# Set places for the norms' transposes in a two-layer transformer block: pairs, a second queue for the first group's reads, and dummy matmuls at the start

## The chip, the cores and the metric

The kernel runs on one core of a Trainium2 chip. The metric is the device time of one execution in microseconds (us); the number given for a kernel is the median of its runs. The engines are TensorE (matmuls, transposes), VectorE, ScalarE, GpSimd and SyncE, which issues transfers. ScalarE and GpSimd can issue transfers too. In the profile they are called PE (PEld is its weight load), DVE, ACT, POOL and SP; a "q" behind the name marks the issuing of transfers.

## The reference

Two layers, each an attention block and an MLP, with shared weights. The sequence has 2048 rows of 512 numbers, 32 heads of 16, a hidden width of 1792.

```python
def attn(x, wqkv, wo):                      # on the normed x
    qkv = (x @ wqkv).reshape(B, S, 3, H, Dh).transpose(2, 0, 3, 1, 4)
    q, k, v = qkv[0], qkv[1], qkv[2]
    p = softmax(einsum("bhqd,bhkd->bhqk", q, k) * Dh ** -0.5)
    o = einsum("bhqk,bhkd->bhqd", p, v)
    return o.transpose(0, 2, 1, 3).reshape(B, S, D) @ wo

def mlp(x, w1, b1, w2):                     # on the normed x; Mish
    h = x @ w1 + b1
    return (h * tanh(softplus(h))) @ w2

for layer in range(2):
    x = x + attn(layernorm(x), wqkv, wo)
    x = x + mlp(layernorm(x), w1, b1, w2)
```

## The kernel before

The 2048 rows are cut into NCH = 4 chunks of CW = 512. Each layer has three stages.

**Projections** (`qkv`, `v_parts`). The normed chunk is needed transposed (512 features in four blocks of 128 partitions). To keep precision, an operand is split into a high part (a copy by ScalarE) and a low part (a subtraction), and a product is three matmuls (`mm3`, L176 to L178): high by high, low by high, high by low, for each of four blocks, twelve matmuls for one projection of 128 output rows by 512 columns. There are 32 projections (m, c) per layer: m = 0 to 3 are q, m = 4 to 7 are k, c is the chunk. Their order is the list `order`. Each goes into one of three PSUM banks with the tag "s"; ScalarE and VectorE empty it into `pt` (`split_psum`, L170 and L171), and ScalarE issues a write of 512 KB to `scr` in DRAM (L479). The v products follow, interleaved with the first maxima of the attention.

**Norms** (`norm_parts`). For a chunk: statistics of four tiles (`bn_stats`, `bn_aggr`, L191 and L192, VectorE), the power -0.5 (L188, GpSimd), and for each tile of 128 rows the scaled `xn` (L204, VectorE), four transposes (L215, TensorE) into a PSUM tile, and the split into `th` and `tl` (L170, L171). In the first layer's projections and for the last chunk of the second layer's, the PSUM tile has the tag "mx", in the MLP "acc" or "s". `xn` takes a buffer with the tag "f" (two), which it shares with the MLP's `hb`. The first layer's norms are written out before the projections, the second layer's last one (`late`) just before the first projection that needs it.

**Attention** (`Attention`). `prep_qk(g)` reads a group of four heads from `scr` into two tiles `ks` and two tiles `qs`: 24 reads of 128 KB (L266) and four small ones of a constant (`minus`, L259). For the first group all 28 are issued at once when the eight projections with m = 0 and 4 are done, half by SP and half by GpSimd. Then a loop of 512 steps works through scores, exponentials, products with v, and the maxima of the next group.

**MLP** (`mlp`). Loop over chunks and 14 blocks f of the hidden width: `hid` makes twelve matmuls and a chain over ScalarE, VectorE and GpSimd (`hb`, `he`, `hr`, `ah`, `al`, L602 to L612), `outp` makes the twelve matmuls of the second product two steps later (LAG = 2). `hooks` puts the norms of other chunks (`spread`), the last output projection (`quarter`) and loads at given (c, f).

The order on an engine is chosen by the tile framework's scheduler, except for instructions pinned by `behind` (they stay in program order) and TensorE's instructions that go through `att.pe` with `chained` set (each depends on the one before). Before, `chained` is set once the first group's reads are issued. Buffers come from pools; an instruction waits until its buffer is free.

Of the kernel before, what the change touches and what calls it, by code (L numbers as in the profile page):

```python
# [43 lines left out]
KEEP = 2  # L44
GSTEPS = NCH * NKT
# [21 lines left out]
def kernel(ctx: ExitStack, tc: tile.TileContext, x, wqkv, wo, w1, b1, w2, out):  # L67
# [23 lines left out]
    nc.sync.dma_start(b1t, b1.rearrange("(f p) -> p f", p=P))  # L91
# [33 lines left out]
    def split_load(key, src, a, b, later, raw=None):  # L125
        t = b8([P, 2, a, b], F32R, "s" + key)
        if raw is None:
            raw = tmp.tile([P, a, b], F32, tag="raw", name="r" + key, bufs=3)
        behind(nc.sync.dma_start(raw, src))

        def split():
            behind(nc.scalar.activation(t[:, 0], raw, AF.Copy))
            behind(nc.gpsimd.tensor_tensor(t[:, 1], raw, t[:, 0].bitcast(F32), op=ALU.subtract))
            unkept.append((key, t))

        later.append(split)
        return t
# [42 lines left out]
    def norm_parts(src, nm, got, key, tag, fine=False, pin=lambda ins: ins, pe=lambda ins: ins, halves=False):  # L180
# [20 lines left out]
        for t in range(NCH):  # L201
            xn = t512("f", f"xn{nm}{t}")
# [7 lines left out]
            if tag == "mx":  # L210
                tp = ps.tile([P, 2, 512], F32, tag=tag, name=f"tp{nm}{t}")[:, 0]
            else:
                tp = pbank(tag, f"tp{nm}{t}")
            for k in range(KT):
                pe(nc.tensor.transpose(tp[:, ts(k, P)], xn[:, ts(k, P)], ident))  # L215
# [3 lines left out]
    def norm(src, nm, got, key, tag, fine=False):  # L219
        for _ in norm_parts(src, nm, got, key, tag, fine):  # L220
            pass
# [6 lines left out]
    class Attention:  # L228
# [20 lines left out]
        def prep_qk(self, g):  # L249
            l = self.l  # L250
            ks, qs = [], []
            for u in range(HG // 2):
# [3 lines left out]
                for e in range(2):  # L256
                    r0 = e * HALF
                    queue = nc.gpsimd if g == 0 and e else nc.sync
                    queue.dma_start(  # L259
                        k[r0 + KROWS : r0 + MROWS].bitcast(F32).rearrange("p (r n) -> p r n", n=P),  # L260
                        minus[:, None, :].to_broadcast([MROWS - KROWS, S // P, P]),
                    )
                    yield
                    for t, parts, base in ((k, K_PARTS, NCH), (q, Q_PARTS, 0)):
                        for j, a in enumerate(parts):
                            queue.dma_start(  # L266
                                t[r0 + j * DH : r0 + (j + 1) * DH].bitcast(F32),
                                self.scr[base + m][a, (h0 + e) * DH : (h0 + e + 1) * DH, :].bitcast(F32),
                            )
                            yield  # L270
# [163 lines left out]
    def load_qkv(l, wts, which, later):  # L434
        raw = None
        for j in which:
# [3 lines left out]
            elif j < 4:  # L440
                wts[j] = split_load(key, *cols(wqkv, j), later)
# [5 lines left out]
    def qkv(l, wts, tt, order, late, due):  # L447
        scr = [dram.tile([2, P, S], F32R, name=f"scr{l}{m}") for m in range(2 * NCH)]
        att = Attention(l, scr)
# [9 lines left out]
        spare = []  # L459
        for n, (m, c) in enumerate(order):  # L460
            if c not in tt:
                late()
# [6 lines left out]
            else:  # L469
# [3 lines left out]
            mm3(  # L473
                acc,
                [(w[:, 0, k, ts(m % 2, P)], w[:, 1, k, ts(m % 2, P)], th[:, k], tl[:, k]) for k in range(KT)],
                pe=att.pe,
            )
# [20 lines left out]
        return att  # L498
# [90 lines left out]
    def mlp(l, x2s, w1t, w2t, tts, dst, hooks):  # L589
        acts, obs = {}, {}  # L590

        def hid(c, f):
# [62 lines left out]
    wts, tt, late = {}, {}, None  # L655
# [11 lines left out]
    load_qkv(0, wts, (0, 2), splits)  # L667
    xc.append(load_x(1))
    for c in range(NCH):
        parts = norm_parts(xc[c], f"q0{c}", tt, c, "mx", c == 0)  # L670
        next(parts)
        if c == 0:
            split_all(splits)
        for _ in parts:
            pass
        if c + 2 < NCH:
            xc.append(load_x(c + 2))
    for l in range(2):
        due = {}
        if l == 0:  # L680
# [8 lines left out]
        att = qkv(l, wts, tt, order, late, due)  # L689
# [80 lines left out]
        for c in range(NCH - 1):  # L770
            spread(hooks, [(c, f) for f in (range(8, 13) if c == 0 else range(5, 10))], x2s[c + 1], f"m{l}{c + 1}", tts, c + 1)
# [8 lines left out]
        if l == 0:  # L780
            late = lambda: norm(x2s[last], f"q1{last}", tt, last, "mx", True)
# [29 lines left out]
```

## Time and profile before

| | |
|---|---|
| median of 3 runs | 3584.75 us (3584.71 to 3588.09) |
| profiled execution | 3589.2 us, of which its span 3587.4 us |
| TensorE busy | 3540.3 us, 99% of the span |
| VectorE, ScalarE, GpSimd busy | 83%, 70%, 15% |
| first layer: norms and projections | 0 to about 145 us |
| first layer: attention, output projection | to about 1468 us |
| first layer: MLP | 1469 to about 1827 us |
| second layer: projections | from about 1800 to 1970 us |
| second layer: attention, output projection | to about 3250 us |
| second layer: MLP and end | to 3587.4 us |

How to read the profile: times are microseconds from the span's start. In a timeline, a line has the start, the time, the engine, the source line, the operation, output <- input, and in brackets the idle time of the engine before it and what ended that. A windows table gives for each stretch its length, then for each engine the busy time and the number of instructions, the granted clock of TensorE, and the mean share of the 16 DMA engines that was busy. A matmul's listed time contains its drain; in a stream, the distance of the starts is what it costs. Idle time of an engine that does not set the end costs nothing.

### The profile page before, as it was taken

What the parts mean: (1) busy time and instruction counts of PE and PEld (TensorE: products, weight loads), DVE (VectorE), ACT (ScalarE), POOL (GpSimd) and SP (SyncE); (2) the same over time, 40 slices, a digit from 0 to 9 for tenths busy, and PEclk for the clock granted to TensorE, in tenths of its full rate; (3) what the DMA queues carried; (4) which work ended last, traced back from release to release, by engine and by line L of the source; (5) the groups of instructions that cost most, each with busy time, mean ns of one, the idle gap of its engine ahead of it and who ended that gap; (6) DMA issues with size and microseconds to landing.
All of it is one profiled execution on the core that took longest, in us unless ns stands there. A gap on an engine that the chain in (4) does not pass through costs nothing.

```text
span 3587.4 us, 69160 instructions
## 1 busy us (share of the span) xinstructions
PE 3540.3 (99%) x28704; PEld 1942.6 (54%) x28704; DVE 2967.9 (83%) x3042; ACT 2518.1 (70%) x3411; POOL 550.4 (15%) x591
## 2 busy tenths in 40 slices
PE   7999999999999999999999999999999999999999
PEld 5644444444444444778776444444444444448887
DVE  4779999999999994666648799999999999946565
ACT  2178888888888888344421788888888888873444
POOL 2200000000010002444421000000000000024455
PEclk9999999999999999999999999999999999999999
DMA  6561322213121224500164312112021221245000
GB/s 193 195 170 39 81 54 68 61 46 79 45 67 51 52 79 70 181 36 13 47 183 165 70 32 40 32 41 38 26 47 29 46 38 29 79 73 178 36 12 24
DMA packets 139457, 255.11 MB, mean 71 GB/s; under 512 B 29432, under 2 KB 73336, under 8 KB 125320
## 3 DMA queue, kind: packets, MB, share of 16 engines
q1 hardware_dynamic: 112648, 175.64, 19.8%
q0 software_dynamic: 8224, 35.21, 3.5%
q10 hardware_dynamic: 18272, 39.85, 3.0%
q8 instruction: 225, 3.69, 0.5%
q14 instruction: 88, 0.72, 0.1%
HBM read 149.43 MB, written 100.14 MB: 70 GB/s over the span
## 4 chain that ended last, share of the span: by engine, by line
PE 49%; DVE 1%; DMA 1%; ACT 1%; issue 0%; POOL 0%; POOLq 0%; DVEq 0%; ACTq 0%; SPq 0%
PE pv L377 15%; PE pm L303 9%; PE ss L361 6%; PE sp L351 5%; PE mo L178 2%; PE h L176 2%; PE h L178 2%; PE h L177 2%; PE mo L176 2%; PE mo L177 2%; PE qk L176 1%; PE qk L178 1%; PE qk L177 1%; PE va L176 0%; DMA ks<-scr 0%
## 5 line engine op out<-in xcount | busy, mean ns | idle before, releaser
L307 DVE TENSOR_REDUCE mxv<-pm 128x2 f32<-128x1024 f32 x2048 | 2386.0, 1218 | 138.4 <-PE pm L303 87.6
L352 ACT ACTIVATE p<-sp 128x1024 f32<-128x1024 f32 x1366 | 1395.8, 1022 | 20.1 <-PE sp L351 14.1
L377 PE MATMUL pv<-p,va 128*32 128x256 f32 (+2 forms) x16032 | 1167.0, 392 | 0.1
L303 PE MATMUL pm<-ks,qs 48*128 48x512 f32 x4096 | 1097.1, 447 | 0.3
L362 ACT ACTIVATE p<-ss 128x512 f32<-128x512 f32 x1364 | 814.6, 597 | 348.5 <-PE ss L361 264.7
L351 PE MATMUL sp<-qs,ks 50*128 50x512 f32 x2732 | 726.5, 447 | 0.3
L377 PEld LDWEIGHTS pv<-p,va 128*32 128x32 f32 x16032 | 368.4, 109 | 498.3 <-issue 420.7
L303 PEld LDWEIGHTS pm<-ks,qs 48*128 48x128 f32 x4096 | 450.6, 184 | 345.1 <-issue 210.8
L361 PE MATMUL ss<-qs,ks 50*128 50x512 f32 x1364 | 611.3, 448 | 0.0
L361 PEld LDWEIGHTS ss<-qs,ks 50*128 50x128 f32 x1364 | 252.2, 185 | 329.3 <-ACT p L362 224.1
L351 PEld LDWEIGHTS sp<-qs,ks 50*128 50x128 f32 x2732 | 261.8, 183 | 200.8 <-ACT p L352 119.5
L322 POOL CAST np<-nt 128x32 fp32r<-128x32 f32 x64 | 13.3, 208 | 2214.2 <-DVE nt L320 2214.2
L608 POOL TENSOR_TENSOR hb<-hb,he 128x512 f32<-128x512 f32 x112 | 157.6, 1407 | 193.0 <-DVE he L605 189.0
L611 POOL TENSOR_TENSOR hb<-hb,hr 128x512 f32<-128x512 f32 x112 | 159.8, 1427 | 138.5 <-DVE ah L610 130.8
L606 ACT ACTIVATE hr<-he 128x512 f32<-128x512 f32 x112 | 70.8, 633 | 149.9 <-POOL hb L611 76.8
L612 DVE TENSOR_TENSOR al<-hb,ah 128x512 fp32r<-128x512 f32 x112 | 107.9, 963 | 81.9 <-POOL hb L611 80.5
L170 ACT ACTIVATE pt<-qk 128x512 fp32r<-128x512 f32 x64 | 37.9, 598 | 159.5 <-PE qk L178 133.5
L604 ACT ACTIVATE he<-he 128x512 f32<-128x512 f32 x112 | 70.8, 632 | 100.1 <-DVE he L603 97.0
L602 ACT ACTIVATE hb<-h,b1t 128x512 f32<-128x512 f32 x112 | 76.7, 685 | 77.0 <-DVE al L612 46.9
L610 DVE TENSOR_TENSOR ah<-hb,hr 128x512 fp32r<-128x512 f32 x112 | 76.9, 687 | 60.3 <-ACT hr L607 42.6
L605 DVE SCALAR_TENSOR_TENSOR he<-he 128x512 f32<-128x512 f32 x112 | 79.9, 714 | 42.0 <-ACT he L604 39.4
L603 DVE TENSOR_SCALAR he<-hb 128x512 f32<-128x512 f32 x112 | 69.7, 622 | 49.4 <-POOL hb L608 36.7
(224 smaller groups left out, 3246.7 us busy)
## 6 DMA issues: line engine op xcount, KB each, us to landing
scr<-pt ACTq DMA_DIRECT2D x64, 512.0 KB
qs<-scr SPq DMA_DIRECT2D x180, 128.0 KB
ks<-scr SPq DMA_DIRECT2D x180, 128.0 KB
vscr<-v SPq DMA_DIRECT2D x32, 512.0 KB
va<-vscr SPq DMA_DIRECT2D x64, 256.0 KB
oscr<-ot SPq DMA_DIRECT2D x64, 256.0 KB
ww<-sw POOLq DMA_DIRECT2D x14, 1024.0 KB, 4.5
num<-oscr SPq DMA_DIRECT2D x64, 128.0 KB
```

Of the source, the lines that this page charges most:

```text
L176: pe(nc.tensor.matmul(acc, ah, bh, start=first and i == 0, stop=False))
L177: pe(nc.tensor.matmul(acc, ah, bl, start=False, stop=False))
L178: pe(nc.tensor.matmul(acc, al, bh, start=False, stop=last and i == n - 1))
L303: nc.tensor.matmul(pm[:, e], qs[u][rows, q0 : q0 + P], ks[u][rows, ts(n, 512)], start=True, stop=True)
L307: nc.vector.tensor_reduce(self.mxs[b][:, 2 * u : 2 * u + 2, qt, n], pm, axis=AX.X, op=ALU.max)
L351: self.pe(nc.tensor.matmul(sp[:, e], k, q, start=True, stop=True))
L352: nc.scalar.activation(self.pts[-1][:, 0:n], sp[:, 0:n], AF.Exp, scale=SCALE)
L361: self.pe(nc.tensor.matmul(sp, k, q, start=True, stop=True))
L362: nc.scalar.activation(self.pts[i // 3][:, 2], sp, AF.Exp, scale=SCALE)
L377: nc.tensor.matmul(self.accs[b][ts(h, VW), cols], self.va[b // NCH][:, kt, h, :], self.pts[j][:, e, cols], start=kt == 0 and q0 == 0, stop ...
L608: nc.gpsimd.tensor_tensor(hb, hb, e, op=ALU.mult)
L611: nc.gpsimd.tensor_tensor(hb, hb, r, op=ALU.mult)
```

## The change

- `norm_parts` with the tag "mx" first makes all four `xn` (two in "f", two in "ah"), then transposes tiles in pairs into both halves of a PSUM tile, and splits a pair by one ScalarE and one VectorE instruction. With the tag "acc" `xn` takes a buffer with the tag "raw".
- The first layer's norms 1 to 3 and the second layer's last norm are called piece by piece at set places (n, k) of the projections, n counting them and k the four blocks inside one. TensorE's instructions are chained from the start of each layer's projections. The second layer's order has one more projection, (5, 1), before (0, 3).
- `prep_qk(0)` issues the 14 transfers of the first pair of heads at once (half by SP, half by GpSimd), the 14 of the second by ScalarE, pinned, two behind each of the next seven projections.
- Four dummy matmuls of zeros (f32, 128 x 512) before the first norm's transposes, three after them.
- The low parts of the first two weight tiles are made by VectorE instead of GpSimd; all of x is loaded right after them; `b1t` is loaded behind x.
- In the MLP the norm of chunk 1 lies at f = 0 to 4 instead of 8 to 12; the transposes of chunk 0's MLP norm lie two to five steps later in the output projections; in the last two f of the last chunk VectorE does two products that GpSimd did.

```diff
+PREP = 7
+WARM = (4, 3)
...
+        def scaled(t, tag):
+            if tag == "raw":
+                xn = tmp.tile([P, 2, 512], F32, tag=tag, name=f"xn{nm}{t}", bufs=3)[:, 0]
+            else:
+                xn = t512(tag, f"xn{nm}{t}")
             pin(
                 nc.vector.tensor_scalar(
                     xn, src[:, t], mv[:, t, 0:1], rs[:, t : t + 1], op0=ALU.subtract, op1=ALU.mult
                 )
             )
+            return xn
+
+        if tag == "mx":
+            xns = [scaled(t, ("f", "ah")[t // 2]) for t in range(NCH)]
+            yield
+            for u in range(NCH // 2):
+                tp = ps.tile([P, 2, 512], F32, tag=tag, name=f"tp{nm}{u}")
+                for e in range(2):
+                    for k in range(KT):
+                        pe(nc.tensor.transpose(tp[:, e, ts(k, P)], xns[2 * u + e][:, ts(k, P)], ident))
+                two = ts(u, 2 * P)
+                split_psum(
+                    th[:, :, two].rearrange("p k (t n) -> p k t n", n=P),
+                    tl[:, :, two].rearrange("p k (t n) -> p k t n", n=P),
+                    tp.rearrange("p t (k n) -> p k t n", n=P),
+                    pin,
+                )
+                yield
+            return
+        for t in range(NCH):
+            xn = scaled(t, "raw" if tag == "acc" else "f")
...
-                    queue = nc.gpsimd if g == 0 and e else nc.sync
-                    queue.dma_start(
+                    queue = nc.sync
+                    pin = lambda ins: ins
+                    if g == 0 and u:
+                        queue, pin = nc.scalar, behind
+                    elif g == 0 and e:
+                        queue = nc.gpsimd
+                    pin(queue.dma_start(
...
-            if c not in tt:
-                late()
+            for fn in within.get((n, 0), []):
+                fn()
...
+            for k in range(KT):
+                for fn in within.get((n, k), []) if k else []:
+                    fn()
+                mm3(
...
             for fn in due.get((m, c), []):
                 fn()
+            for _ in range(2):
+                next(parts, None)
             if m in (0, 4):
                 done += 1
                 if done == 2 * NCH:
-                    for _ in att.prep_qk(0):
-                        pass
-                    att.chained = True
+                    parts = att.prep_qk(0)
+                    for _ in range(2 * PREP):
+                        next(parts)
...
-            nc.gpsimd.tensor_tensor(hb, hb, e, op=ALU.mult)
+            mul = nc.vector if (l, c) == (1, NCH - 1) and f >= FT - 2 else nc.gpsimd
+            mul.tensor_tensor(hb, hb, e, op=ALU.mult)
...
-            nc.gpsimd.tensor_tensor(hb, hb, r, op=ALU.mult)
+            mul.tensor_tensor(hb, hb, r, op=ALU.mult)
...
-    load_qkv(0, wts, (0, 2), splits)
-    xc.append(load_x(1))
-    for c in range(NCH):
-        parts = norm_parts(xc[c], f"q0{c}", tt, c, "mx", c == 0)
-        next(parts)
-        if c == 0:
-            split_all(splits)
-        for _ in parts:
-            pass
-        if c + 2 < NCH:
-            xc.append(load_x(c + 2))
+    load_qkv(0, wts, (0, 2), splits, nc.vector)
+    xc += [load_x(c) for c in range(1, NCH)]
+    nc.sync.dma_start(b1t, b1.rearrange("(f p) -> p f", p=P))
+    att = attention(0)
+    att.chained = True
+    norms = [norm_parts(xc[c], f"q0{c}", tt, c, "mx", c == 0, behind, att.pe) for c in range(NCH)]
+    warm = b8([P, CW], F32, "warm")
+    nc.vector.memset(warm, 0.0)
+
+    def warm_up(i, n):
+        acc = pbank("s", f"warm{i}")
+        for _ in range(n):
+            att.pe(nc.tensor.matmul(acc, warm[:, 0:P], warm, start=True, stop=True))
+
+    warm_up(0, WARM[0])
+    for i in range(4):
+        next(norms[0])
+        if i > 1:
+            splits.pop(0)()
+    warm_up(1, WARM[1])
...
+            for c, (n0, n1, n2) in enumerate(((0, 0, 2), (2, 3, 5), (4, 6, 7)), 1):
+                for at in ((n0, 0), (n1, 0), (n2, 1), (n2, 3)):
+                    within.setdefault(at, []).append(lambda c=c: next(norms[c]))
         else:
-            order = [(0, 0), (0, 1), (0, 2), (4, 0), (4, 1), (4, 2), (1, 0), (1, 1), (1, 2), (5, 0), (0, 3), (4, 3)]
+            order = [(0, 0), (0, 1), (4, 0), (4, 1), (1, 0), (0, 2), (4, 2), (1, 1), (1, 2), (5, 0), (5, 1), (0, 3), (4, 3)]
+            att = attention(1)
+            att.chained = True
+            late = norm_parts(x2s[NCH - 1], f"q1{NCH - 1}", tt, NCH - 1, "mx", True, pe=att.pe)
+            for at in ((4, 0), (4, 0), (9, 0), (9, 2)):
+                within.setdefault(at, []).append(lambda: next(late))
...
-            for n in range({0: 1, 6: 1, 9: 2, 12: 2, 15: 2}.get(i, 0)):
+            for n in range({0: 1, 8: 1, 11: 2, 14: 2}.get(i, 0)):
                 next(first)
         for i, _ in enumerate(project(2)):
-            if i == 1:
+            for n in range({1: 2, 6: 1}.get(i, 0)):
                 next(first)
...
-            spread(hooks, [(c, f) for f in (range(8, 13) if c == 0 else range(5, 10))], x2s[c + 1], f"m{l}{c + 1}", tts, c + 1)
+            spread(hooks, [(c, f) for f in (range(5) if c == 0 else range(5, 10))], x2s[c + 1], f"m{l}{c + 1}", tts, c + 1)
...
-            late = lambda: norm(x2s[last], f"q1{last}", tt, last, "mx", True)
```

More of the change, by code (lines that the diff above doesn't have):

```diff
@@ L123, in keep, with split_load @@
         behind(nc.gpsimd.dma_start(kept[key].bitcast(F32), t.bitcast(F32)))
-    def split_load(key, src, a, b, later, raw=None):
+    def split_load(key, src, a, b, later, raw=None, low=nc.gpsimd):
         t = b8([P, 2, a, b], F32R, "s" + key)
@@ L132, in split @@
             behind(nc.scalar.activation(t[:, 0], raw, AF.Copy))
-            behind(nc.gpsimd.tensor_tensor(t[:, 1], raw, t[:, 0].bitcast(F32), op=ALU.subtract))
+            behind(low.tensor_tensor(t[:, 1], raw, t[:, 0].bitcast(F32), op=ALU.subtract))
             unkept.append((key, t))
@@ L432, in run, with load_qkv @@
             open_banks()
-    def load_qkv(l, wts, which, later):
+    def load_qkv(l, wts, which, later, low=nc.gpsimd):
         raw = None
@@ L445, in load_qkv, with attention, qkv @@
                 wts[j] = split_load(key, *rows2(wqkv[:, 2 * D : 3 * D], j - 4), later, raw[:, j - 4])
-    def qkv(l, wts, tt, order, late, due):
-        scr = [dram.tile([2, P, S], F32R, name=f"scr{l}{m}") for m in range(2 * NCH)]
-        att = Attention(l, scr)
+    def attention(l):
+        return Attention(l, [dram.tile([2, P, S], F32R, name=f"scr{l}{m}") for m in range(2 * NCH)])
+    def qkv(l, att, wts, tt, order, within, due):
+        scr = att.scr
         ahead = [0]
@@ L653, in load_x @@
         return xc
-    wts, tt, late = {}, {}, None
+    wts, tt = {}, {}
     splits, later = [], []
```

37 lines of the change are left out of this document (14 added, 23 removed).

## The prediction

> **What bounds the kernel now.** I read the page, then the windows of the projection stages, then the timeline and the chain where TensorE idles.
>
> ```profile
> span 3587.4 us, 69160 instructions
> PE 3540.3 (99%) x28704; PEld 1942.6 (54%) x28704; DVE 2967.9 (83%) x3042; ACT 2518.1 (70%) x3411; POOL 550.4 (15%) x591
> ```
>
> TensorE bounds it: all its idle time together is 3587.4 - 3540.3 = 47.1 us. The change removes no matmul of the result, so it can win only those 47.1 us and the slow matmuls behind idle stretches.
>
> ```profile
> core 0: us, PE busy (x) PEld busy (x) DVE busy (x) ACT busy (x) POOL busy (x), PEclk, DMA share, GB/s
> 33.00:51.00 18.00, 12.81 (x57) 9.83 (x57) 12.20 (x27) 6.04 (x12) 1.77 (x2) 0.81 0.10 36
> 81.20:90.30 9.10, 4.89 (x13) 3.83 (x13) 1.98 (x3) 3.57 (x5) 3.84 (x3) 0.63 1.04 173
> 1750.00:1800.00 50.00, 47.25 (x213) 36.16 (x212) 27.42 (x50) 23.82 (x38) 20.77 (x17) 1.00 0.12 43
> 1840.00:1850.00 10.00, 7.33 (x29) 5.46 (x29) 4.37 (x7) 2.77 (x5) 0.00 (x0) 0.75 0.27 105
> 1870.00:1880.00 10.00, 7.39 (x33) 5.76 (x32) 2.08 (x3) 2.06 (x4) 1.89 (x2) 1.00 1.02 256
> ```
>
> The idle time lies in five places: 13.1 us in the first 20 us (windows 0 to 10 and 10 to 20), 5.5 at 33 to 51, 4.2 at 81 to 90, 7.4 over the first layer's MLP (1460 to 1840), 5.3 at 1840 to 1880. The two attention loops, 160 to 1400 and 1980 to 3180, have almost none, and the program built from the changed kernel has TensorE's order unchanged in them.
>
> ```profile
> 17.17 1.65 PE L176 MATMUL qk<-thq,sqkv 128*128 128x512 f32 x3 [0.69 <-ACT thq L170]
> 37.10 1.09 PE L215 MATMUL tpq<-ident,xnq 128*128 128x128 f32 x4 [2.34 <-DVE mvq L192]
> 83.57 0.37 ACTq L479 DMA_DIRECT2D scr<-pt  x1
> 85.41 0.80 PE L176 MATMUL qk<-thq,sqkv 128*128 128x512 f32 x1 [4.21 <-DVE pt L171]
> 1799.66 0.50 PE L176 MATMUL qk<-thq,qkv0l 128*128 128x512 f32 x1 [0.33 <-ACT hb L602]
> 1844.44 1.68 PE L215 MATMUL tpq<-ident,xnq 128*128 128x128 f32 x8 [1.99 <-DVE tlq L171]
> 1860.45 11.46 DMA ks<-scr
> 1873.78 0.50 PE L176 MATMUL qk<-thq,qkv1l 128*128 128x512 f32 x1 [2.61 <-DVE pt L171]
> 3580.34 0.50 PE L178 MATMUL mo<-w26l,al 128*128 128x512 f32 x1 [0.90 <-DVE al L612]
> ```
>
> The brackets give the wait and its releaser. Transposes wait for a norm (37.10, 1844.44); projections wait for a bank that ScalarE and VectorE have not emptied (85.41, 1873.78), because ScalarE stood before issuing a write (83.57; its evacuation at 73.08 was the last before) while the first group's 24 reads of ks and qs crowd the DMA engines. After idle stretches matmuls step by 0.43 us instead of 0.227 for some 4.9 us (85.41 to 90.27): 12 of them lose 12 x 0.2 = 2.4 us.
>
> **Start and the first layer's norms.** Before, the first qk matmul runs at 17.17 and full speed begins at 22.31, when 11 are done: as if a full-speed run began at 22.31 - 11 x 0.227 = 19.8. After, I lay the built order end to end: x's last tile is reduced as now by 9.0, less 0.45 for the b1t issue that SP no longer makes first (row at 0.74), so the four xn (0.46 apart) end at 10.6. The first pair goes through transposes and ScalarE by 11.4, the weights' high part (1.06) by 12.4, the second pair by 13.5. VectorE does tl (1.22, taken from L587's 128x1024 row), the weights' low part (1.2 by the same row; GpSimd took 2.49 each), and the second tl by 15.1. Full speed from 14.9: 4.9 won.
>
> The dummies are f32 of 512 columns. The nearest row is pv 128x512 f32, 1.06 us with its drain: some 0.85 to 1.06 us at full step, 1.7 at half, so the first four run from about 1.3 to 7.2, and the transposes come at 9.2, 2.0 us later. Whether the speed survives is open: 1.99 us idle lost it at 1844.44 (eight transposes 1.68 us against 1.04), 2.61 us at 1871 to 1873.78 did not. If lost, transposes and the three later dummies run slow and full speed starts at 16.0: 3.8 won. I take 4.4.
>
> The Trainium skill ("TensorE: Matmul & The Clock Gate", Part 1: The HAM clock gate) says that the clock falls back only after at least one idle window of about 3.4 us, free-running. By that rule the 2.0 us would keep the speed and the gain would be 4.9; the 1.99 us row speaks against the rule as stated.
>
> From 17.17 to 81.2 TensorE does 17 projections, 204 x 0.227 = 46.3, and 48 transposes at 0.13, 6.2: 52.5 of 64.0 us. So 11.5 are lost, 2.6 of them the start above (19.8 - 17.17); 8.9 remain. After, norms 1 to 3 are placed at projections 0 to 7, transposes four steps of TensorE ahead of use. VectorE then carries, per chunk, statistics 2.46 + 0.5, xn 1.9, tl 2.5, and 0.69 per projection: 3 x 7.4 + 9 x 0.69 = 28.3 us inside nine projections with transposes (9 x 2.72 + 6.2 = 30.7). That nearly fills it. Laid end to end, chunk 1's first xn comes at 22.9 when TensorE arrives at 21.0: a wait of 1.9, and behind it (TensorE is in order) stand all projections. Later ones fit. Gain 8.9 - 1.9 = 7.0; 4.6 if that wait also brings the slow step back (2.4), 8.9 if there is no wait. The rows of 1.99 and 2.61 us leave this open; I take off a quarter of the 2.4: 6.4.
>
> **The reads.** Before: 4.2 idle + 2.4 slow at 81 to 90, and 2.6 at 1873. After, half of the 28 issues (24 reads, 4 of minus) are made at once by SP and GpSimd, the other 14 by ScalarE, two after each of the next seven projections, pinned in its order. An issue costs ScalarE some 0.37 (the ACTq row): 14 x 0.37 = 5.2 us in seven projections of 2.72 (19.0), beside evacuation and write, 7 x 1.0; it has room. Queued behind a waiting read are the evacuation of the next projection and its write; TensorE has two spare banks, 5.4 us. In the built program each transfer waits for the one eight before it. Reads cost the DMA engines about 0.7 us each (70 to 80: 2.22 MB at share 0.93, less about 1 MB of writes at the 395 GB/s of the window 17.17 to 22.31), two plus a write of 512 KB (1.3) make 2.7 us per projection: just as much as there is. So ScalarE will be held now and then; I expect 0.5 to 1 us lost per layer. Gain (6.6 - 1) + (2.6 - 0.5) = 7.7; ends 0 and 9.2, and below nothing by rival 1.
>
> **Second layer's last norm.** Its statistics move ahead of projection 4, its transposes into projection 9, so nothing waits: the 1.99 + 0.69 idle, 0.6 of slow transposes and 11 slow matmuls (2.2) go: 5.5, with 4 as the low end if two transposes wait.
>
> **MLP.** xn takes its buffer from "raw" instead of the two "f" buffers of hb. The 0.33 us waits for hb, one per step in the last chunk (1766 to 1800), are hb waiting for a buffer. TensorE loses 7.4 us over this MLP, with 0.6 to 1.4 us waits for al among them, which stay. The first chunk's norm now lies at f 0 to 4, beside num and ol (2.3 to 2.5 us each on VectorE), where there was no TensorE idle in 1460 to 1540: cover that it may use up. I take 3.5 of 7.4, from -2 to 6. In the second layer 0.7 (the wait at 3338), from -1.
>
> **Rest.** Transposes of chunk 0's MLP norm are moved two to five steps later in the output projections: waits of 0.59 + 0.56 and 0.63 + 0.56: 1.5 of 2.3; no loss, since nine of project(2)'s sixteen steps of 0.68 us still lie between the last and the first h. Tail: two products by VectorE (0.69 after ah's row) instead of GpSimd (1.30) in the last two f: up to 0.9, the wait at 3580.34, down to -0.5, since VectorE now does them in series; I take 0.6, nearer the row. Norm transposes in pairs halve the count of ScalarE and VectorE instructions but not their elements: nothing.
>
> **Sum.** 4.4 + 6.4 + 7.7 + 5.5 + 3.5 + 0.7 + 1.5 + 0.6 = 30.3 us. The profiled execution took 3589.2 (span 3587.4 + 1.8), 0.12% above the median of 3584.75; differences in span carry over, so from the median: 3584.75 - 30 = 3555. All low ends: 3.8 + 4.6 + 0 + 4 - 2 - 1 + 0 - 0.5 = 8.9, so 3576; all high: 4.9 + 8.9 + 9.2 + 5.5 + 6 + 0.7 + 2.3 + 0.9 = 38.4, so 3546.
>
> **Rivals.** (1) ScalarE's reads block its evacuations, and the kernel gets slower. Before, SP needed 16.08 us for six reads of ks (1860.10), 2.7 each. At that price 14 reads take ScalarE 38 us, with its own 7 a total of 45 against a cover of 19.0 + 5.4: TensorE loses 20 us a layer and 2.4 of slow steps, 45 in both layers, in place of the 9.2 lost now. The other gains are 30.3 - 7.7 = 22.6, so 3584.75 - 22.6 - 9.2 + 45 = 3598. It turns the sign from 2 x loss - 9.2 = 22.6, a loss of 16 us a layer, 2.2 us a read. Against it: those six stood behind all 24 issued in 5 us; now they come two per projection. 6%. (2) The reads take just as long and the same gaps stay (7.7 lost from the sum): 3562. For it: the DMA share is already 1.04 at 81 to 90, and the bytes are the same. 15%. The Trainium skill ("DMA: Bandwidth & Descriptors", Issuing engines are not separate DMA queues) says that transfers of all issuers run on the same 16 engines and another issuer saves only issue time; by that rule alone this rival would be the forecast, but the spreading in time is not an issuer's doing. (3) VectorE becomes the bound: the wait of 1.9 cools the array and recurs at chunks 2 and 3 (6.4 becomes 0), and the MLP gives nothing (3.5): 3565. 15%. (4) The dummies do not keep the clock: only the 0.6 between 4.4 and 3.8. This is inside the forecast.
>
> **Numbers.** Forecast 3555, chance 60%; (2) and (3) 15% each, (1) 6%, about no change 4%. From 3546 to 3572 holds the forecast, (2), (3) and most sums with several low ends; left out are (1), no change and the ends together. 0.2%, 7.2 us, is about what a measurement here tells from no change: faster 0.90, same 0.04, slower 0.06.
>
> **What would show it.** First qk matmul at full step by 15 to 16 us; no gap over 2 us at 33 to 51; no gap over 1 us at 70 to 95, and ScalarE's idle there under 5 us at a time; no transposes waiting at 1840; hb's 0.33 waits gone. It is wrong if ScalarE stands over 10 us in front of a read, or if the MLP's idle grows.

## The result and the profile after

The changed kernel takes 3556.12 us (median of 6 runs, 3554.26 to 3558.21), the kernel before 3585.06 in the same comparison (6 runs, 3583.44 to 3588.09): a ratio of 0.9917, 95% interval 0.9905 to 0.993, 28.9 us less. The forecast was 3555, the range 3546 to 3572. The profiled execution of the changed kernel took 3554.46.

The page of the changed kernel, span and busy times:

```profile
span 3552.7 us, 69170 instructions
PE 3531.6 (99%) x28718; PEld 1938.4 (55%) x28718; DVE 2963.1 (83%) x3039; ACT 2520.7 (71%) x3401; POOL 521.6 (15%) x571
```

TensorE's idle time is 3552.7 - 3531.6 = 21.1 us, where it was 47.1. Its busy time fell by 8.7 although the dummies add 8.1 of it: fewer matmuls run at the slow step (0.43 us from start to start, where the full step is 0.227), and short delays, which count as busy, went too (see the first MLP below).

The windows of the changed kernel, at the places of the forecast and at one that the forecast had not named (1515 to 1530; the row 70 to 90 covers the forecast's 81 to 90):

```profile
core 0: us, PE busy (x) PEld busy (x) DVE busy (x) ACT busy (x) POOL busy (x), PEclk, DMA share, GB/s
33.00:51.00 18.00, 18.00 (x95) 15.18 (x94) 12.04 (x20) 7.02 (x10) 1.77 (x2) 1.00 0.44 166
70.00:90.00 20.00, 19.34 (x85) 13.80 (x84) 10.32 (x12) 4.62 (x8) 6.22 (x3) 1.00 0.82 290
1515.00:1530.00 15.00, 12.17 (x49) 9.50 (x48) 5.69 (x10) 3.58 (x6) 5.04 (x5) 0.89 0.70 280
1750.00:1800.00 50.00, 50.00 (x233) 41.02 (x232) 32.53 (x58) 21.01 (x34) 19.45 (x17) 1.00 0.37 141
1840.00:1850.00 10.00, 10.00 (x45) 6.89 (x44) 4.44 (x6) 2.48 (x5) 1.81 (x1) 1.00 0.98 311
```

The idle time of 33 to 51, of the MLP's last chunk and of 1840 is gone, and 0.66 us are left at 70 to 90. New is 1515 to 1530, with 2.83 us idle and a granted clock of 0.89.

The timeline of the changed kernel (start, duration, then engine, line and tiles; in brackets the wait and its releaser):

```profile
1.46 5.35 PE L713 MATMUL warm<-warm 128*128 128x512 f32 x8 [1.46 <-DVE warm L708]
8.59 2.02 PE L222 MATMUL tpq<-ident,xnq 128*128 128x128 f32 x16 [1.78 <-DVE xnq L209]
14.35 0.51 PE L178 MATMUL qk<-tlq,sqkv 128*128 128x512 f32 x1 [0.92 <-DVE tlq L172]
22.32 1.11 PE L222 MATMUL tpq<-ident,xnq 128*128 128x128 f32 x8 [1.78 <-DVE xnq L209]
...
1516.06 0.32 SPq L161 DMA_DIRECT2D w24l<-ww  x1
1520.87 0.80 PE L177 MATMUL mo<-w24l,ah 128*128 128x512 f32 x1 [2.05 <-DMA w24l<-ww]
1521.46 0.63 PE L178 MATMUL mo<-w24l,ah 128*128 128x512 f32 x1
```

The four first dummies stand as eight records (x8): a matmul of these f32 operands is recorded twice, and the records step by 0.85 us at first and by 0.43 from 4.93 on. The 16 transposes take 2.02 us after a wait of 1.78 (3.41 in e3, which has no dummies): TensorE kept its full speed over that wait. Chunk 1's first xn makes TensorE wait 1.78 us at 22.32, and the steps behind it are full too. At 1520.87 the second matrix of the MLP (mo) waits for block 4 of w2 (w24l), which SP issued only at 1516.06, and then runs five slow steps; the second layer repeats it (2.02 at 3287.42).

To see where the time went, the run is cut at TensorE's first matmul of certain tiles (sp opens an attention loop, h an MLP). TensorE has the same matmuls between these marks in both kernels, apart from the seven dummies; times are of the profiled executions.

| stretch | before | after | gained | forecast |
|---|---|---|---|---|
| start to first sp | 186.7 | 168.3 | 18.4 | 4.4 + 6.4 + 5.6 = 16.4 |
| first sp to first h (layer 1) | 1282.4 | 1280.6 | 1.8 | 0.75 |
| first h to first sp of layer 2 | 500.9 | 484.8 | 16.1 | 3.5 + 5.5 + 2.1 = 11.1 |
| first sp to first h (layer 2) | 1282.3 | 1280.7 | 1.6 | 0.75 |
| first h of layer 2 to the end | 335.1 | 338.3 | -3.2 | 0.7 + 0.6 = 1.3 |

The sum is 34.7 by the profiles and 28.9 by the medians: the profiled execution of before (3589.2) lay 4.1 above its median and that of the changed kernel 1.7 below. So the column "gained" holds 5.8 us that are not the change's.

### The profile page after: what moved, and what is told of

Its sections match the earlier page's. It is cut to its first block, busy times and chain, and to the rows that moved or that the text cites. A ratio compares the mean times of both kernels' runs of the same rounds, so it can differ in the third digit from the quotient of the medians.

```text
span 3552.7 us, 69170 instructions
## 1 busy us (share of the span) xinstructions
PE 3531.6 (99%) x28718; PEld 1938.4 (55%) x28718; DVE 2963.1 (83%) x3039; ACT 2520.7 (71%) x3401; POOL 521.6 (15%) x571
## 4 chain that ended last, share of the span: by engine, by line
PE 95%; DMA 2%; DVE 1%; issue 1%; ACT 1%; POOL 1%; ACTq 0%; SPq 0%; DVEq 0%; POOLq 0%
PE pv L401 30%; PE pm L327 17%; PE ss L385 13%; PE sp L375 10%; PE mo L179 3%; PE mo L177 3%; PE mo L178 3%; PE h L179 3%; PE h L177 3%; PE h L178 3%; PE qk L177 1%; PE qk L178 1%; PE qk L179 1%; PE va L177 1%; PE wo L177 1%
## 5 line engine op out<-in xcount | busy, mean ns | idle before, releaser
L642 POOL TENSOR_TENSOR hb<-hb,he 128x512 f32<-128x512 f32 x110 | 149.2, 1356 | 190.3 <-DVE he L638 186.2
L645 POOL TENSOR_TENSOR hb<-hb,hr 128x512 f32<-128x512 f32 x110 | 150.5, 1368 | 139.5 <-DVE ah L644 134.7
L171 ACT ACTIVATE pt<-qk 128x512 fp32r<-128x512 f32 x64 | 37.8, 597 | 148.4 <-PE qk L179 109.9
L646 DVE TENSOR_TENSOR al<-hb,ah 128x512 fp32r<-128x512 f32 x112 | 88.3, 789 | 32.5 <-POOL hb L645 32.3
```

The lines of the kernel that those rows point to most:

```text
L642: mul.tensor_tensor(hb, hb, e, op=ALU.mult)
L645: mul.tensor_tensor(hb, hb, r, op=ALU.mult)
```

## The experiments

Every run was compared with the kernel before on the same chip; the median of the kernel before lay between 3584.91 and 3586.22 in these comparisons, so a difference of 1 us between two experiments says little. "First sp" and the other stretches are those of the table, and read from one execution each. In tile names, th and tl are the high and low part of a normed chunk, ah and al those of the MLP's activation, h its first product, mo its second, wo the output projection.

**e1: the MLP norm of chunk 1 where it was.**

```diff
-            spread(hooks, [(c, f) for f in (range(5) if c == 0 else range(5, 10))], ...)
+            spread(hooks, [(c, f) for f in (range(8, 13) if c == 0 else range(5, 10))], ...)
```

> The changed kernel, with the MLP norm of chunk 1 put back at f 8 to 12 (the change has it at f 0 to 4); xn stays in the raw buffers. In the changed kernel TensorE waits 2.05 us at 1520.87 for the load of w2 block 4 and then runs some nine steps of 0.43 us, and the same again at 3287 in the second layer. Theory A (buffers): taking thm and tlm of chunk 1 at f 1 uses up two of the 22 blocks, so the load of w2 block 4 must wait for the blocks of wo, which the last output projection reads until 1516. With the norm later the load is issued some 20 us earlier as it was before the change (1494), both stalls vanish with their slow steps: first h to first sp from 484.8 to about 480.5 us, second layer's first h to the end from 338.3 to about 334, total 3556 - 8.5 = 3547.5. Theory B (the load is late for the traffic or its order on SP's queue, whatever the norm does): the stalls stay, 3556. Theory C (VectorE): the norm at f 8 to 12 makes h wait for hb there, and 2 to 4 us per layer come back in place of the stalls: 3553 to 3558.

Measured: 3551.31 (ratio 0.9902, 0.9887 to 0.9917). SP's row for the load in this kernel (times in ns, then first and last start):

```profile
L161 SPq DMA_DIRECT2D w24l<-ww x1: 320/320/320, 1473.8 to 1473.8; - x1
```

The load is issued at 1473.8 instead of 1516.06, and no wait for w24l is left in either layer: theory A. SP's waits between 1460 and 1530 say what the load waited for, in the changed kernel:

```profile
SPq L161 <- PE wo L179: 35.6, 2, 34.7
```

The 34.7 us before 1516.06 end with the last output projection (it goes from wo0l to wo1l at 1515.86). e1 has the same wait, but one load later, before block 5:

```profile
L161 SPq DMA_DIRECT2D w25l<-ww x1: 319/319/319, 1515.7 to 1515.7; - x1
```

There TensorE does not feel it. Only 4.8 of the 8.5 us came: the stretches are 482.3 (484.8 in the changed kernel) and 336.4 (338.3). In the second layer 1.5 us of waits for ah and al stand near 3300 where the norm now lies, which is theory C in part; in the layer-2 projections this execution also waited 0.72 for a bank (a PSUM bank that is not yet emptied), the changed kernel's not.

**e2: xn of the spread norms in hb's buffers.**

```diff
-            xn = scaled(t, "raw" if tag == "acc" else "f")
+            xn = scaled(t, "f")
```

> The changed kernel, with xn of the MLP's spread norms back in the two f buffers of hb. Theory A (buffer): hb's wait for a buffer returns, one wait of about 0.33 us (0.5 from start to start) per step in the last chunk of the first layer's MLP: first h to first sp from 484.8 to about 492 us (before, the steps of 1740 to 1820 lost some 8.7 us from start to start), the second layer's MLP up by under 1; total about 3564. Theory B (VectorE's load in the last chunk, three norms beside the activations, makes the waits, whatever the buffer; moving the norm of the last chunk into the projections took them away): no change, 3556.

Measured: 3575.32 (0.9971, 0.996 to 0.9981), 19.2 above the changed kernel. The waits of TensorE in this kernel, 1450 to 1990 (us in total, times, longest):

```profile
PE h L177 <- ACT hb L635: 3.7, 8, 1.5
PE mo L177 <- DMA w24l<-ww: 3.4, 1, 3.4
PE mo L179 <- DVE al L646: 2.7, 2, 2.4
```

hb's waits return, so theory A, but more than twice its price: with the norm at f 0 to 4, xn also holds hb's buffers when the MLP starts (waits of 1.45 for hb and 2.36 for al near 1485), and the wait for w24l grows from 2.05 to 3.44.

**e3: no dummies (and the last products on GpSimd).**

```diff
-WARM = (4, 3)
+WARM = (0, 0)
...
-            mul = nc.vector if (l, c) == (1, NCH - 1) and f >= FT - 2 else nc.gpsimd
+            mul = nc.gpsimd
```

> The changed kernel without the seven dummy matmuls, and with the last two products of hb on GpSimd again (the tail, read by itself at the end of the trace). Theory A (the dummies warm the clock): the 16 transposes of the first norm take about 0.21 us each in place of 0.126 (1.3 us more), and the first projections step by 0.43 for what is left of about 5 us: first sp from 168.3 to about 171; the tail gives back 0.9, the wait for al at the last mo; total 3556 + 2.7 + 0.9 = 3559.6. Theory B (the arrival of x and VectorE's chain set the start, so the clock is worth nothing): first sp stays at 168.3 and the total is 3557.

Measured: 3561.12 (0.9929, 0.9914 to 0.9944). The start of this kernel:

```profile
8.56 3.41 PE L222 MATMUL tpq<-ident,xnq 128*128 128x128 f32 x16 [8.56 <-DVE xnq L209]
13.50 0.50 PE L177 MATMUL qk<-thq,sqkv 128*128 128x512 f32 x1 [1.53 <-ACT thq L171]
15.17 0.80 PE L178 MATMUL qk<-tlq,sqkv 128*128 128x512 f32 x1 [1.16 <-DVE tlq L172]
```

The transposes take 3.41 us in place of 2.02 from the same start (8.56 and 8.59), and the projections then make six steps of 0.43, so theory A. The twelfth matmul of the projections comes at 19.06 instead of 16.75, 2.3 later, but the first sp at 169.7, only 1.4 later: in the changed kernel TensorE runs at full speed into the waits for tlq (0.92 at 14.35) and for chunk 1's xn (1.78 at 22.32), and without the dummies this last wait is covered (no wait at 22.71). The wait for al at the tail is back with 0.8. This execution also had a wait for a bank of 2.18 us with slow steps at 1843.80, which the changed kernel's did not have. It is not the dummies' doing: e9, which has them, waits 2.12 at the same place.

**e4: all steps of the norms at first use.**

```diff
-            for c, (n0, n1, n2) in enumerate(((0, 0, 2), (2, 3, 5), (4, 6, 7)), 1):
-                for at in ((n0, 0), (n1, 0), (n2, 1), (n2, 3)):
+            for c, n0 in enumerate((4, 7, 9), 1):
+                for at in ((n0, 0), (n0, 0), (n0, 0), (n0, 0)):
...
-            for at in ((4, 0), (4, 0), (9, 0), (9, 2)):
+            for at in ((11, 0), (11, 0), (11, 0), (11, 0)):
```

> The changed kernel, with all four steps of norms 1 to 3 of the first layer at the projection that first uses them (places 4, 7 and 9), and of the second layer's last norm too (place 11); pairs, pinned order, reads and dummies as in the changed kernel. Theory A (the place, not the pairs, is the gain): each of the three chunks has TensorE wait for statistics and xn on VectorE (4.9 us), a pair of transposes and its two evacuations (about 3), most of it uncovered, and slow steps behind it: 7 to 10 us a chunk, first sp from 168.3 to 190 to 198; in the second layer 4 to 8 us; total 3580 to 3594. Theory B (VectorE's work of 28.3 us in 30.7 bounds this stretch wherever the norms stand, and the pairs save instructions): under 5 us in all, 3556 to 3561.

Measured: 3597.44, slower than before (1.003, 1.0018 to 1.0041). First sp at 204.0. Its timeline:

```profile
31.81 3.68 PE L222 MATMUL tpq<-ident,xnq 128*128 128x128 f32 x16 [6.50 <-DVE xnq L209]
54.34 3.65 PE L222 MATMUL tpq<-ident,xnq 128*128 128x128 f32 x16 [6.64 <-DVE xnq L209]
```

Each chunk waits 6.5 us for xn, transposes at the slow step, and waits another 1.6 to 1.9 for thq and tlq: 12 us a chunk, above the 7 to 10 expected. Theory A: the place is the gain. The second layer's stretch from first h to first sp lost 4.9.

**e5: the reads issued as before.**

```diff
-PREP = 7
+PREP = 14
...
-                    if g == 0 and u:
-                        queue, pin = nc.scalar, behind
-                    elif g == 0 and e:
+                    if g == 0 and e:
                         queue = nc.gpsimd
```

> The changed kernel with the first group's 28 issues as they were before the change: all at once, alternately on SP and GpSimd, none on ScalarE. Theory A (spreading them in time keeps ScalarE's evacuations going): the waits for a bank come back, about 4 us and 2 of slow steps at some 75 to 85 us and 2 to 4 in the second layer's projections: first sp from 168.3 to 174, first h to the second first sp from 484.8 to 488, total 3556 + 8.5 = 3564.5. Theory B (the bytes set the time and the issuer saves issue time only): waits within 1 us of the changed kernel's, 3556 to 3558.

Measured: 3570.15 (0.9956, 0.994 to 0.9973), 14.0 above the changed kernel: first sp 171.1 (168.3), first h to first sp 498.6 (484.8). ScalarE's row in this kernel:

```profile
1854.00 0.60 ACT L171 ACTIVATE pt<-qk 128x512 fp32r<-128x512 f32 x1 [17.32 <-DMA scr<-pt]
```

ScalarE stands 17.3 us in front of issuing a write (issued at 1853.53) while the 28 transfers run, and TensorE waits 12.9 us for a bank. Theory A, and the second layer costs much more than the 2.6 us that the same issues cost before; why is open.

**e6: ScalarE's reads at once.**

```diff
-PREP = 7
+PREP = 14
```

> The changed kernel with ScalarE's 14 issues made at once, in place of two after each of seven projections. Theory A (spreading is what pays; a read waits for the one eight before it, so 14 in a row hold ScalarE some 14 x 1.3 us or more, against two spare banks of 2.7 us each): TensorE waits 10 to 20 us for a bank in each layer, with slow steps behind it: total 3580 to 3600. Theory B (what pays is that another queue issues them): within 2 us of the changed kernel, 3554 to 3558.

Measured: 3583.35 (0.999, 0.9981 to 0.9999), 27 above the changed kernel. Waits of ScalarE, 60 to 110:

```profile
ACT pt L171 <- DMA ks<-scr: 17.0, 1, 17.0
```

ScalarE stands 17.0 us in the first layer and 20.4 in the second, TensorE 10.9 and 14.3 us for a bank. Theory A: ScalarE as an issuer alone is worth nothing (e5, without it, is 13 us faster), it is the spreading.

**e7: single transposes in place of pairs.** Two tiles, each with its own bank pair and evacuation, at each place of a pair:

```diff
             for u in range(NCH // 2):
-                tp = ps.tile([P, 2, 512], F32, tag=tag, name=f"tp{nm}{u}")
-                for e in range(2):
...
+                for t in (2 * u, 2 * u + 1):
+                    tp = ps.tile([P, 2, 512], F32, tag=tag, name=f"tp{nm}{t}")[:, 0]
...
```

> The changed kernel, with the four norms of the projections transposed and evacuated one 512-column tile at a time, two at the places where the changed kernel does a pair. Theory A (pairs halve the instructions, not the elements, and the path has only fixed costs of 0.1 to 0.2 us more per evacuation): first sp within 0.5 to 2 us of 168.3, total 3556 to 3559. Theory B (pairs are what lets VectorE keep up at 28.3 of 30.7 us): the wait of 1.78 us at chunk 1 grows over 3 and comes back at chunks 2 and 3: total 3562 or more.

Measured: 3564.51 (0.9939, 0.9924 to 0.9954), 8.4 above the changed kernel; first sp at 176.2. Its timeline:

```profile
9.10 1.11 PE L222 MATMUL tpq<-ident,xnq 128*128 128x128 f32 x8 [2.38 <-DVE xnq L209]
11.17 1.74 PE L222 MATMUL tpq<-ident,xnq 128*128 128x128 f32 x8 [0.96 <-DVE tlq L172]
28.63 1.97 PE L222 MATMUL tpq<-ident,xnq 128*128 128x128 f32 x8 [3.46 <-DVE tlq L172]
```

The total is theory B's, the mechanism neither's. The tag has two buffers of two halves each. A pair fills both halves of one, so a norm of two pairs needs two buffers and does not wait for its own evacuations; a single tile takes a whole buffer too, and the third waits until VectorE has emptied the first (tlq). After 0.96 us of that (2.38 of waiting for xn lie just before) and after 3.46 the next transposes run slow (1.74 and 1.97 against 1.1).

**e8: e1 with chunk 1's transposes later.**

```diff
-                for at in ((n0, 0), (n1, 0), (n2, 1), (n2, 3)):
+                for at in ((n0, 0), (n1, 0)) + (((2, 3), (3, 1)) if c == 1 else ((n2, 1), (n2, 3))):
```

> A version meant to beat the changed kernel: the MLP norm of chunk 1 at f 8 to 12 as in the first experiment (3551.3 there), and the two pairs of transposes of chunk 1 in the first layer two and three quarters of a projection later (places 2 and 3 of projection 2, 3 and 1 of projection 3; the changed kernel has 2 and 1, 2 and 3). Theory A (TensorE waits 1.78 us there only because xn comes late from VectorE, and the two steps of 0.68 us between cover most of it): that wait falls to about 0.4, no new wait before projection 4, total 3551.3 - 1.4 = 3550. Theory B (VectorE is the bound of the stretch, what TensorE does not lose here it loses at the next chunk's transposes or for a bank): the 1.4 us come back within the next four projections, 3551.

Measured: 3555.27 (0.9914, 0.9899 to 0.9929), 4.0 above e1; first sp 172.1 (168.6). Its timeline:

```profile
22.54 1.11 PE L222 MATMUL tpq<-ident,xnq 128*128 128x128 f32 x8 [0.42 <-DVE xnq L209]
31.30 0.50 PE L178 MATMUL qk<-tlq,sqkv 128*128 128x512 f32 x1 [3.06 <-DVE tlq L172]
```

The wait falls to 0.42 as worked out, and 3.06 us, with slow steps behind it, come at projection 4, which needs the last tlq. Theory B, and worse: what TensorE does not wait at 22 it waits at 31. VectorE is the bound of this stretch: in the changed kernel it is busy 16.6 of the 18 us from 13 to 31.

**e9: e1 with xn in hb's buffers** (the edits of e1 and e2 together: the MLP as it was before).

> The first experiment's kernel (MLP norm of chunk 1 at f 8 to 12, 3551.3) with xn of the spread norms in hb's f buffers: the MLP as it was before the change. Theory A (the buffer of xn is worth what the steps of before lost from start to start, some 10 us in the first layer, where the page showed 7.4 of idle): first h to first sp from 482.4 to 491 to 493 us, total 3560 to 3563. Theory B (the buffer matters only beside the norm at f 0 to 4, where e2 lost 19): first h to first sp within 2 of 482.4, total 3552 to 3554.

Measured: 3558.25 (0.9921, 0.9907 to 0.9936), 6.9 above e1; first h to first sp 492.3 against e1's 482.3, of which 1.4 is a wait for a bank that is longer here. So theory A: in this placement the buffer is worth 8.6 us in the first layer of these two executions, 6.9 in all by the medians, where brackets for hb in the last chunk show only this (waits of 1740 to 1800 in e9):

```profile
PE h L177 <- ACT hb L635: 1.6, 5, 0.3
```

**e10 and e12: the reads alone, in the kernel before**, with the same queues and pins as the change. e10 lets ScalarE issue two after each projection, e12 one (`next(parts, None)` once, and the tiles of the group entered before the loop, as in e11 below).

```diff
+            for _ in range(2):
+                next(parts, None)
...
-                    for _ in att.prep_qk(0):
-                        pass
+                    parts = att.prep_qk(0)
+                    for _ in range(14):
+                        next(parts)
```

> The kernel before the change with the reads alone changed: u = 0 on SP and GpSimd at once, u = 1 by ScalarE, two issues after each of the next seven projections, in ScalarE's pinned order. Theory A (the spreading takes away the waits of 4.21 and 2.61 us and the slow steps behind the first): first sp from 186.7 to 181, first h to the second first sp from 500.9 to 498.5, total 3585 - 8 = 3577. Theory B (the reads of the changed kernel were in trouble only for the new order of its norms and projections, as 12.9 us in e5 against 2.6 before suggest; in the old order ScalarE's pinned reads cost as much as they save): within 3 us of 3585.

> The kernel before the change with e10's reads (3585.6, no gain), but one issue by ScalarE after each of the next 14 projections in place of two after each of seven. Theory A (the pace was the trouble in e10: ScalarE stood 4 to 8 us at a time behind transfers and the gain of the spreading was lost to that): with half the pace it does not, the waits for a bank go under 1 us, first sp from 183.3 to about 181, first h to the second first sp from 502.0 to about 497, total 3577 to 3579. Theory B (the old order of norms, whose evacuations share these stretches, makes the waits, whatever the pace): within 3 us of 3585.

Measured: e10 3585.56 (1.0003, 0.9993 to 1.0012), no gain; e12 3577.69 (0.998, 0.997 to 0.999), 8.5 less than before. Waits of ScalarE in e10, 1840 to 1900:

```profile
ACT pt L170 <- DMA ks<-scr: 12.2, 2, 8.3
ACT pt L170 <- DMA scr<-pt: 6.7, 2, 4.3
```

In e10 ScalarE stands up to 8.3 us behind its own reads and up to 4.3 behind a write, and TensorE waits for a bank 3.2 us beside the reads of the first layer and 2.2 in the second. In e12 ScalarE's longest stand behind a transfer in these stretches is this one, between 1820 and 1900:

```profile
ACT pt L170 <- DMA qs<-scr: 4.0, 1, 4.0
```

TensorE has no wait for a bank beside the reads of either layer there. Theory A of e12: the pace.

**e11: e1 with one read per projection.** The tiles of the group are entered before the loop, so that the maxima of u = 0 can start while reads of u = 1 are still to be issued; that moves no instruction by itself.

```diff
-            ks, qs = [], []
+            ks, qs = self.qk[g] = [], []
...
-            for _ in range(2):
-                next(parts, None)
+            next(parts, None)
```

> A version meant to beat the changed kernel: the first experiment's (3551.3) with one of ScalarE's reads after each of the next 14 projections instead of two after each of seven. Theory A (what is left of waits for a bank, 1.3 us in the first layer, 1.0 in the second and more in some executions, is ScalarE standing behind a transfer): they fall under 0.5 each, first sp 168.6 to 167.5, total 3549 to 3550 and a smaller spread of times. Theory B (these waits are the 14 reads issued at once by SP and GpSimd, and come whatever ScalarE does): same waits, 3551.

Measured: 3547.03 (4 runs, 3546.09 to 3547.89), ratio 0.9891, 0.9874 to 0.9907: the fastest kernel of this study, 9.1 us below the changed one and 38 below the one before. Its windows, and ScalarE's waits at 60 to 110:

```profile
60.00:90.00 30.00, 30.00 (x135) 22.82 (x133) 13.76 (x17) 8.36 (x13) 7.83 (x6) 1.00 0.89 261
1820.00:1860.00 40.00, 40.00 (x178) 30.04 (x177) 21.43 (x25) 7.78 (x13) 10.18 (x10) 1.00 0.79 244
```

```profile
ACT pt L171 <- PE qk L179: 37.0, 15, 3.1
```

TensorE has no idle time in either stretch, and between 60 and 110 no evacuation of ScalarE waits for a transfer (in the changed kernel 4.3 and 2.4 us); in the second layer those of the projections wait 2.9 and 2.0 us, where the changed kernel's waited up to 6.1. The DMA engines are as busy as ever (0.89). Theory A; the 14 reads that SP and GpSimd issue at once do no harm.

## Why the prediction was right, and where its terms were not

The first and third stretch of the table can be cut finer, at matmuls of the projections before and after which both kernels have the same matmuls: the 12th and the 204th of the first layer, the 72nd and the 204th of the second. Again from the two profiled executions:

| term | before | after | gained | forecast |
|---|---|---|---|---|
| start, to the 12th | 22.31 | 16.75 | 5.6 | 4.4 |
| norms 1 to 3, 12th to 204th | 58.50 | 50.95 | 7.5 | 6.4 |
| reads, 204th to first sp | 105.9 | 100.6 | 5.3 | 5.6 |
| first MLP, first h to the 72nd | 361.1 | 353.2 | 7.9 | 3.5 |
| last norm, 72nd to 204th | 37.8 | 31.8 | 6.0 | 5.5 |
| second layer's reads, 204th to first sp | 102.0 | 99.8 | 2.2 | 2.1 |

**Start (4.4).** The mechanism held, dummies included. The term that was short is x's arrival: the first statistics start at 3.40, before the change at 5.03, 1.6 us earlier where 0.45 was put for SP's order. The order was not tried by itself, and the arrival varies: e10 and e12, with the start of before, begin them at 4.31 and 4.28. The wait after the dummies was 1.78 (forecast 2.0) and kept the full speed, the end that the Trainium skill's rule ("TensorE: Matmul & The Clock Gate", Part 1: The HAM clock gate) gave. The dummies themselves are worth 1.4 us (e3).

**Norms 1 to 3 (6.4).** The wait for chunk 1's xn is 1.78 where 1.9 was worked out. e4 and e8 show VectorE's chain as the bound that the step named: the steps have to be early, and TensorE's wait cannot be moved away. Of the 7.5 us, 2.7 are chance: e10 and e12, whose norms are those of before, need 55.8 there in place of 58.5, because no slow steps followed their wait of 2.34. So the gain is 4.8 to 7.5. The sentence that pairs are worth "nothing" was wrong: e7 costs 8.4. It counted instructions and elements and did not count buffers.

**The reads (7.7).** In the changed kernel they behave as forecast (0.66 us of waits in the first layer, none in the second; 5.3 + 2.2 gained). But the worth is not one number: taking them out costs 14.0 (e5), putting them alone into the kernel before brings nothing (e10), and 8.5 at half the pace (e12). The forecast compared the changed kernel's waits with those of before, and so had the difference right and the reason half: it asked whether ScalarE has time for two issues per projection, 5.2 us of 19.0, and the reads' duration; the pace decides whether ScalarE stands. Rival 1's mechanism is thus real (17.0 and 20.4 us in e6, 8.3 in e10) and was avoided by a small margin: in the changed kernel ScalarE stood 2.4 us behind a transfer at 70 to 95, where the forecast named 5, but 4.3 just before (to 66.76) and 6.1 in the second layer. Rival 2 is wrong for the changed kernel and describes e10. The Trainium skill ("DMA: Bandwidth & Descriptors", Issuing engines are not separate DMA queues) says that another issuer saves issue time only; that is in line with e5 and e6, where ScalarE as a further issuer made the kernel 13 us slower, and no run here shows the issue time that it saves.

**Second layer's last norm (5.5).** Nothing waits for the late norm, as forecast. But 2.7 of the 6.0 us are chance again: e12 has the wait of 1.99 of before and no slow steps behind it, and needs 35.1 for the stretch in place of 37.8. The forecast priced the slow steps of one profile as a fixed cost.

**First MLP (3.5).** This is the term that was mis-sized most, in both directions. From before to e9 the stretch falls by 2.6 (361.1 to 358.5), which no run takes apart; from e9 to e1, xn's buffer alone, by 8.6; from e1 to the changed kernel, the norm at f 0 to 4, it rises by 3.3. The price of hb's waits was taken from the idle time of the page (7.4, of which half). But a bracket begins where the modelled end of the matmul before lies (0.39 us behind its start), 0.16 us later than the next start would be: a bracket of 0.33 costs 0.49 from start to start, and delays under 0.16 show no bracket at all. From 1740 to 1800 the windows of before show 3.4 us idle, and its starts lose about 7 against a step of 0.2265; in the changed kernel about 1. Against it stands what the forecast had only as a sign ("cover that it may use up"): the norm at f 0 to 4. Not num and ol were in its way but the 22 blocks: two more are held from f 1, so w2's block 4 waits, 2.05 us and slow steps.

**Second layer's MLP (0.7).** It lost about 4 (table, less the tail's gain), with the wrong sign; "from -1" was too narrow. Some 2 of it are the wait for w24l (338.3, and 336.4 in e1 without it); the rest is in e1 too, with 1.5 us of waits for ah and al. "Wrong if the MLP's idle grows" came true here: 3.6 us of brackets where before had 1.7.

**Chunk 0's norm (1.5)** gave 1.8 + 1.6: waits and their hidden 0.16 us each make 3.0 of it. **Tail (0.6):** the wait of 0.90 is gone, and back with 0.8 in e3.

**Sum.** 30.3 was forecast, 34.7 is the difference of the two profiles and 28.9 that of the medians; 5.8 us lie between, and the 2.7 + 2.7 us of slow steps above are of that size. Terms too small (start, the MLP's buffer, chunk 0's norm) and a missed cost (w24l twice) offset each other. That the total came within 1.4 us is luck in part: it is better than its parts.

## What to carry to other kernels

When an engine that evacuates banks also issues DMAs, the pace of the issues counts, not their sum: one read per projection was free, two cost 4.3 us (e1 against e11) and 7.9 (e12 against e10), fourteen at once cost 11 us in the first layer and 15 in the second (e6). Taking a pool's buffers earlier has a price elsewhere: look which later load gets the buffer that is now last to come free. And sum TensorE's losses from start to start, not from the brackets.

## What was not expected of the hardware

Whether TensorE loses its full step after an idle stretch is not settled by the stretch's length between 1.94 and 2.61 us. The same wait for w24l, 1.98 us long, is followed by slow steps in e5 and by full ones in e6:

```profile
1523.40 0.51 PE L177 MATMUL mo<-w24l,ah 128*128 128x512 f32 x1 [1.98 <-DMA w24l<-ww]
1524.22 0.63 PE L177 MATMUL mo<-w24l,ah 128*128 128x512 f32 x1
1524.65 0.63 PE L178 MATMUL mo<-w24l,ah 128*128 128x512 f32 x1
```

```profile
1531.39 0.50 PE L177 MATMUL mo<-w24l,ah 128*128 128x512 f32 x1 [1.98 <-DMA w24l<-ww]
1532.19 0.39 PE L177 MATMUL mo<-w24l,ah 128*128 128x512 f32 x1
1532.42 0.40 PE L178 MATMUL mo<-w24l,ah 128*128 128x512 f32 x1
```

The wait of 1.99 for the late norm lost the speed before and kept it in e12:

```profile
1833.75 1.23 PE L215 MATMUL tpq<-ident,xnq 128*128 128x128 f32 x8 [1.99 <-DVE tlq L171]
```

Likewise 1.94 (e5, second layer) and 2.05 lost it, 2.34 at chunk 1 lost it before and not in e10 and e12, and 2.61 kept it before. At the two ends the traces agree: 1.78 kept the speed wherever it stood, and 3.06 and more lost it (e8, e7, e4). What decides in between is open. Executions of one program differ with it: in e12 those with a mean granted clock of 1.000 took 3574.0 to 3576.2, those with 0.998 3581.7 to 3585.3. e11, with no wait over 1.8 us, varies by 1.8 in 4 executions, e12 by 11.3 in 9. A slow stretch in one profile is thus a chance of some 1.5 to 2.7 us (1520.87 in the changed kernel; the late norm of before against e12), not a fixed cost.
